# Backward attention loop: dQ of two query chunks packed in one PSUM bank by key tiles with zero columns, and a new loop order

## The chip, the cores and the metric

The kernel runs on one core of one Trainium2 chip. A core has a matrix engine (TensorE, PE in the profile), a vector engine (DVE), an activation engine (ACT), a general engine (POOL) and a queue engine that only issues DMAs (SP). PE writes its results into PSUM, eight banks of 128 partitions x 512 fp32. The metric is the device time of one execution in microseconds; the profile is one execution.

## The reference

One transformer block, forward and backward, for a sequence of 2048 tokens with 512 features, in bf16: layer norm with modulation, self-attention with 32 heads of 16 features, output projection, a second layer norm and an MLP with squared ReLU; then the gradients of the input, the weights and the modulation for a given `grad_out`. The core of what matters here:

```python
qkv = (x @ wqkv).reshape(B, S, 3, H, Dh) ...          # H = 32, Dh = 16
scores = jnp.einsum('bhqd,bhkd->bhqk', q, k) * Dh ** (-0.5)
p = _softmax(scores, axis=-1)
o = jnp.einsum('bhqk,bhkd->bhqd', p, v)
...
_out, _vjp = jax.vjp(_f, A_x, A_wqkv, A_wo, ...)
_grads = _vjp(grad_out)
```

In the backward pass of the attention, with P the softmax and dO the gradient at its output, dV = P^T dO, dS = P * (dO V^T - delta), dK = dS^T Q and dQ = dS K.

## The kernel before

The program runs in stages: preparation of q, k and v; the forward attention with the dense layers of finished query chunks in between; the dense backward layers of the last chunk; the backward attention loop (lines 1557 to 1776), to which the change belongs; and a last stage that turns and multiplies the gradients (lines 1778 to 1998). Tensors between the stages are kept in DRAM: `q_st` holds q by groups of four heads, `k_st` (line 89) holds k by tokens, all heads side by side.

The backward loop works on eight groups of four heads. Within a group it goes through four chunks of 512 keys (kc), and within each through four chunks of 512 queries (qc); one such pair is a block, 128 blocks in all. A block is four units of 128 queries. For a unit and a head:

- `score` (line 1596, token s): one matmul makes 128 x 512 scores in one of three PSUM banks, called A, B and C. Its operands use 32 of PE's rows; the four heads of a group lie on four different groups of rows.
- `expo` (line 1606, token e): ACT takes the exponential from the bank into E_u.
- `dp_pair` (line 1611, token D): for two heads at once, two matmuls make dO V^T - delta in psD_u, a pair of banks (two such pairs exist), and DVE multiplies by E_u into dS_u. This is a product in what follows; a block has eight.
- `k_quad` and `v_quad` (lines 1657 and 1666, token q): four matmuls each add the unit to dK and dV in one bank, accVK.
- `transpose_unit` (line 1632): for dQ the products must be turned. SP issues DMA transposes of dS_u into dsT: for two units at a time (line 1640, 1.05 MB), and in odd blocks for units 0 and 1 at a time and for unit 2 alone (line 1638, half the size). Unit 3 of odd blocks is turned by PE instead (`pe_turn`, line 1649, tokens t) and copied by ACT (tokens T, line 1769).
- `dq_quad` (line 1682, token d): for each of the four key tiles of a block, four matmuls, one per head, multiply the turned products with k. The weights are 32 columns of KS_tok, which holds k by tokens for all heads: 16 columns of the head and the 16 columns after them. So each head's 32 rows of the bank (dqacc, which takes bank C's place) hold 16 rows of dQ and 16 rows that nobody reads.
- `dq_out` (line 1693, token Q): ACT copies the bank out; for the first key chunk to dQacc (line 1700), for later ones to dqtmp (line 1703), which POOL adds (line 1708). At a head group's end its dQ is stored by four DMAs (line 1712).

The order of the work is written out by hand. Two lists of tokens (lines 1714 to 1722), one for iterations after an odd block (`order_t`) and one for the others (`order_n`), are played in turn; the letters beside them give the bank of each score. The order of the tokens sets the order on each engine; engines run their own lists in order and wait for each other by semaphores. The counters nD and nq (line 1732) say which product and which quad a D or q token stands for; nD starts at -1, so products lag one token behind. An iteration b does the scores of block b, turns the PE part of block b-1, and multiplies dQ of block b-2. PE also gets small dummy matmuls (`keep_warm`, line 1645, token f).

ACT's queue also issues DMAs: `plan_head` (line 1587) spreads the loads of the next head group over the loop, one every four products, and stores go the same way. POOL spreads q of the next group into place (`spread_qz`, line 1221). KS_tok is filled once, ahead of the loop, by four DMAs (lines 1370 to 1373).

Of the kernel before, what the change touches and what calls it, by code (L numbers as in the profile page):

```python
# [20 lines left out]
P = 128  # L21
# [8 lines left out]
EPS = 1e-5  # L30
QPAD = 528


@with_exitstack
def kernel(
# [111 lines left out]
    with ExitStack() as ph:  # L147
# [848 lines left out]
        def plan_tasks():  # L996
# [72 lines left out]
            def token_tile(which, g, ti):  # L1069
                key = (which, g)  # L1070
                if ti == 0:
                    T[key] = cb.tile([P, 4, D], BF, name="tokP", tag=htags[(g if which == 0 else g + 1) % 3])
                t = 4 * g + ti
                pt = pools["mm"].tile([P, 4, P], BF, name="ptk", tag="pm")
                for b in range(4):
                    src = sP[:, 4 + 4 * (g % 2) + b, ti * P:(ti + 1) * P] if which == 0 else KTs[b][:, t * P:(t + 1) * P]
                    PE.transpose(pt[:, b, :], src, identb[:])
                gs = slice(4 * g, 4 * g + 4)
                if which == 1:
                    DVE.tensor_copy(T[key][:, ti, :], pt.rearrange("p b q -> p (b q)"))  # L1080
                    if ti == 3:
                        later(1, sp, k_st[:, gs, :], T[key][:])
                else:
                    tok = T[key].rearrange("p t d -> p (t d)").rearrange("p (g t e) -> p g t e", g=HG, t=4)
                    DVE.tensor_copy(tok[:, :, ti, :], pt.rearrange("p b q -> p (b q)").rearrange("p (g e) -> p g e", g=HG))
                    if ti == 3:
                        later(1, sp, q_st.rearrange("g p t e -> p g t e")[:, :, gs, :], tok)

# [132 lines left out]
        def spread_qz(hg):  # L1221
# [3 lines left out]
            else:  # L1225
                POOL.tensor_scalar(to, fro, SCALE, None, ALU.mult)

        def tick():
# [13 lines left out]
        def last_chunk(O_c, L, w1T, w2T):  # L1242
# [301 lines left out]

    KS_tok, dOs_tok = keep["KS"], keep["dOs"]
    qz1pool = tc.alloc_tile_pool(name="qz1pool", bufs=1, side="right")
# [10 lines left out]
    with ExitStack() as ph:  # L1557
# [9 lines left out]
        def load_head(hg):  # L1567
            st = dict(hsets[hg % 2])
            st["qz"] = qz[hg % 2]
            st["acc"] = stg.tile([P, n], F32, name="dQacc", tag="dQacc", bufs=1)  # L1570
            st["dq"] = stg.tile([P, n], BF, name="dQst", tag="dQst", bufs=1)
            st["vk"] = stg.tile([P, n], BF, name="vkb", tag="vkb")
            hst[hg] = st


        todo = {}
# [29 lines left out]
        def expo(u, hq):  # L1606
            if hq == 0:
                bst[u] = [ework.tile([P, 4, 512], BF, name="E_u", tag="E_u"), None]
# [36 lines left out]
        def keep_warm():  # L1645
            PE.matmul(cur["vk"][0:DH, :], KS_tok[:, 0, D:QPAD], dOs_tok[:, 0, :], start=False, stop=False,
                      tile_position=(0, 0), skip_group_check=True)
# [34 lines left out]
        def dq_quad(b, kt):  # L1682
            hg, kc, qc, _ = units[4 * b]
            if kt == 0:
                cur["dq"] = psx.tile([P, 512], F32, name="dqacc", tag="px")
            acc = cur["dq"]
            tT = dqt[b]
            for hq in range(4):
                h = hg * 4 + hq
                PE.matmul(acc[32 * hq:32 * hq + 32, :], KS_tok[:, kc * 4 + kt, h * DH:h * DH + 32], tT[:, :, hq * 4 + kt, :],  # L1690
                          start=(kt == 0), stop=(kt == 3), tile_position=(0, 32 * hq), skip_group_check=True)

        def dq_out(b):
            hg, kc, qc, _ = units[4 * b]
            acc = cur["dq"]
            del dqt[b]
            st = hst[hg]
            dst = st["acc"][:, qc * 512:(qc + 1) * 512]
            if kc == 0:
                ACT.activation(dst, acc[:], AF.Identity, scale=SCALE)  # L1700
            else:
                tmp = wk.tile([P, 512], F32, name="dqtmp", tag="dqtmp")
                ACT.activation(tmp[:], acc[:], AF.Identity, scale=SCALE)  # L1703
                if kc == QC - 1:
                    dst2 = st["dq"][:, qc * 512:(qc + 1) * 512]
                else:
                    dst2 = dst
                POOL.tensor_tensor(dst2, dst, tmp[:], ALU.add)  # L1708
            if kc == QC - 1 and qc == QC - 1 and hg < HG - 1:
                for hq in range(4):  # L1710
                    r = hg % 2 * 64 + hq * DH
                    at(cur["j"] + 6 + hq, load, dQc[hg // 2, r:r + DH, :], st["dq"][32 * hq:32 * hq + DH, :])

        order_t = (
# [3 lines left out]
            "s15 q q e15 ").split(), "ABCABBABACABABCA"  # L1718
# [10 lines left out]
        with tc.manual_schedule(engines={PE.engine, ACT.engine, DVE.engine, SP.engine, POOL.engine}):  # L1729
            head_fill(1)  # L1730
            POOL.memset(qz[1][:], 0.0)
            nD, nq = -1, -4
            idle = psx.tile([P, 512], F32, name="idle", tag="accVK")
            for b in range(NU // 4 + 3):
                toks, bank = order_t if on_pe(b - 1) else order_n
                for tok in toks:
# [38 lines left out]
            assert not todo  # L1775
        dq_last = hst[HG - 1]["dq"]

    with ExitStack() as ph:
# [281 lines left out]
```

## Time and profile before

| | |
|---|---|
| time of the runs, median (lowest to highest) | 2516.67 us (2509.24 to 2526.46), 3 runs |
| profiled execution, span | 2517.6 us |
| PE busy | 2342.5 us, 93% |
| ACT busy | 2302.3 us, 91% |
| DVE busy | 1810.1 us, 72% |
| POOL busy | 350.0 us, 14% |
| first and last exponential of the backward loop | start at 1125.3 and 2379.8 us |
| last dQ matmuls | start at 2389.8 us |

The span is the time from the first to the last instruction of the profiled execution; it is within a microsecond of the median of the runs. Shares are averages over all stages. A PE or ACT instruction overlaps the one after it, so their busy shares say less than the distance between the starts of successive instructions. In a line of the timeline the first number is the start in us from the span's start, the second the length of the instruction or of a merged run of like ones (x3 is three of them), and in brackets stands how long the engine was idle before it and what released it. In a line of the costliest groups stand the number of instructions, the busy time in us, the mean of one in ns, and the idle time before them. SPq and ACTq are the queues' own instructions, such as the issue of a DMA.

### The profile page before, as it was taken

To read this page: it belongs to the slowest core of one execution; us is meant where nothing else is said; L and a number is where in the kernel's file an instruction comes from. 1 tells how busy PE (TensorE), PEld (TensorE's weight loads), DVE (VectorE), ACT (ScalarE), POOL (GpSimd) and SP (SyncE) were. 2 spreads that over 40 slices of the span, in tenths; PEclk is the share of its full clock that TensorE was granted. 3 is DMA by queue.
4 is the path that set the end of the run, shared out by engine and by line. 5 is a ranking of instruction groups with operands and counts; after the bars stand their busy time and mean duration, and the time that the engine had idled before them with its cause. 6 is when DMAs were issued, how large, how long until landed. Compare 5 with 4: busy or idle time off the path is not lost. (4 is left out here: it accounts for less than half of the span.)

```text
span 2517.6 us, 49897 instructions
## 1 busy us (share of the span) xinstructions
PE 2342.5 (93%) x19005; PEld 776.3 (31%) x19005; DVE 1810.1 (72%) x2341; ACT 2302.3 (91%) x3577; POOL 350.0 (14%) x379
## 2 busy tenths in 40 slices
PE   7899889989988999999999999999999999999999
PEld 3232223222322323442233322233323323322343
DVE  5556153454435454579999999999999999998862
ACT  7999999999989999539999999999999999999842
POOL 2000000211323142210111101111010111100100
PEclk9999999999999999999999999999999999998999
DMA  6476455367658766979999999999999999999972
GB/s 202 136 193 165 150 122 139 96 161 144 103 85 176 151 134 119 261 208 191 202 199 210 196 206 208 201 207 202 207 202 202 209 195 203 195 208 212 196 237 72
DMA packets 1220981, 447.15 MB, mean 178 GB/s; under 512 B 1096951, under 2 KB 1191607, under 8 KB 1220486
## 3 DMA queue, kind: packets, MB, share of 16 engines
q1 hardware_dynamic: 1192822, 409.11, 82.2%
q0 software_dynamic: 10944, 16.78, 4.8%
q10 hardware_dynamic: 16976, 18.07, 2.8%
q8 instruction: 149, 2.44, 0.4%
q14 instruction: 90, 0.74, 0.1%
HBM read 96.75 MB, written 73.95 MB: 68 GB/s over the span
## 5 line engine op out<-in xcount | busy, mean ns | idle before, releaser
L1625 DVE TENSOR_TENSOR dS_u<-psD_u,E_u 128x1024 bf16<-128x1024 f32 x1024 | 1186.0, 1218 | 71.6 <-PE psD_u L1623 24.0
L567 ACT ACTIVATE ET<-psST 128x1024 bf16<-128x1024 f32 x1024 | 942.0, 1260 | 27.0 <-PE psST L565 26.5
L1609 ACT ACTIVATE E_u<-psS_A 128x512 bf16<-128x512 f32 x768 | 513.1, 668 | 10.5 <-PE psS_C L1603 8.5
L1609 ACT ACTIVATE E_u<-psS_B 128x512 bf16<-128x512 f32 x768 | 505.8, 659 | 12.1 <-DMA dsT<-dS_u 3.0
L1623 PE MATMUL psD_u<-iv,ido 32*128 32x512 bf16 x2048 | 409.6, 388 | 0.0
L565 PE MATMUL psST<-qt_sb,kt_sb 32*128 32x512 bf16 x2048 | 317.8, 387 | 62.0 <-ACT ET L567 46.6
L1609 ACT ACTIVATE E_u<-psS_C 128x512 bf16<-128x512 f32 x512 | 335.4, 655 | 3.3 <-PE psS_B L1603 1.4
L1603 PE MATMUL psS_B<-ik,iq 32*128 32x512 bf16 x768 | 295.3, 385 | 12.8 <-ACT E_u L1609 5.5
L1603 PE MATMUL psS_A<-ik,iq 32*128 32x512 bf16 x768 | 293.4, 382 | 10.9 <-DVE dwlast L237 1.0
L1603 PEld LDWEIGHTS <-iq 32*128 32x128 bf16 x2048 | 130.2, 91 | 316.1 <-issue 298.8
L1663 PE MATMUL accVK<-dS_u,qz 128*32 128x512 bf16 x2048 | 213.3, 390 | 0.4 <-PE psD_u L1623 0.2
L581 PE MATMUL oacc<-ET,vaug 128*32 128x512 bf16 x2048 | 207.7, 396 | 2.2 <-DVE ostage L585 2.2
L1672 PE MATMUL accVK<-E_u,dOs_tok 128*16 128x512 bf16 x2048 | 204.1, 387 | 0.0
L1708 POOL TENSOR_TENSOR dQacc<-dQacc,dqtmp 128x512 f32<-128x512 f32 x64 | 81.2, 1268 | 852.0 <-ACT dqtmp L1703 852.0
L1603 PE MATMUL psS_C<-ik,iq 32*128 32x512 bf16 x512 | 194.7, 380 | 4.2
L565 PEld LDWEIGHTS <-kt_sb 32*128 32x128 bf16 x2048 | 85.8, 91 | 352.2 <-issue 324.6
L1690 PE MATMUL dqacc<-dsT,KS_tok 128*32 128x512 bf16 x2048 | 146.5, 384 | 18.5 <-DMA dsT<-dS_u 4.3
L1769 ACT ACTIVATE dsT<-ptT 128x1024 bf16<-128x1024 bf16 x128 | 145.8, 1139 | 7.9 <-PE ptT L1653 7.3
L251 DVE COPY part<-pm 128x512 f32<-128x512 f32 (+2 forms) x103 | 63.5, 617 | 114.8 <-PE pm L233 111.5
L1623 PEld LDWEIGHTS <-ido 32*128 32x128 bf16 x2048 | 104.6, 91 | 98.9 <-issue 92.9
L1663 PEld LDWEIGHTS <-qz 128*32 128x32 bf16 x2048 | 58.4, 94 | 177.9 <-issue 162.9
L581 PEld LDWEIGHTS <-vaug 128*32 128x32 bf16 x2048 | 53.1, 93 | 121.4 <-issue 121.4
(407 smaller groups left out, 2516.3 us busy)
## 6 DMA issues: line engine op xcount, KB each, us to landing
p_st<-part POOLq DMA_DIRECT2D x36, 256.0 KB, 5.2
kt_sb<-qkT_st SPq DMA_DIRECT2D x124, 64.0 KB
wA<-in_B_w_dram SPq DMA_DIRECT2D x28, 256.0 KB
wB<-w1T_st SPq DMA_DIRECT2D x21, 256.0 KB
wA<-w2T_st SPq DMA_DIRECT2D x21, 256.0 KB
wB<-in_B_w_dram SPq DMA_DIRECT2D x21, 256.0 KB
p_st<-part POOLq DMA_DIRECT2D x25, 192.0 KB, 5.3
p_st<-part SPq DMA_DIRECT2D x18, 256.0 KB
```

Of the source, the lines that this page charges most:

```text
L565: PE.matmul(ps[:, hi, :], kt_sb[r:r + 32, kt * P:(kt + 1) * P], qt_sb[r:r + 32, :], start=True, stop=True, tile_position=(r, 0))
L567: ACT.activation(ET[:, 2 * pair:2 * pair + 2, :], ps[:], AF.Exp, scale=SCALE)
L581: PE.matmul(oacc[32 * hq:32 * hq + 32, :], lhsT, ET[:, hq, :], start=(kt == 0), stop=(kt == TT - 1), tile_position=(0, 32 * hq), skip_grou ...
L1603: PE.matmul(psS[:], st["q"][r:r + 32, qt * P:(qt + 1) * P], st["k"][r:r + 32, kc * 512:kc * 512 + 512], start=True, stop=True, tile_positi ...
L1609: ACT.activation(bst[u][0][:, hq, :], sst.pop((u, hq))[:], AF.Exp, scale=SCALE)
L1623: PE.matmul(psD[:, hi, :], st["do"][r:r + 32, qt * P:(qt + 1) * P], st["v"][r:r + 32, kc * 512:kc * 512 + 512], start=True, stop=True, til ...
L1625: DVE.tensor_tensor(dS_u[:, 2 * pair:2 * pair + 2, :], psD[:], E_u[:, 2 * pair:2 * pair + 2, :], ALU.mult)
L1663: PE.matmul(cur["vk"][32 * hq:32 * hq + 32, :], hst[hg]["qz"][:, qt, hq, :], bst[u][1][:, hq, :], start=(qt == 0), stop=False, tile_positi ...
L1672: PE.matmul(acc[32 * hq:32 * hq + DH, :], dOs_tok[:, qt, (hg * 4 + hq) * DH:(hg * 4 + hq + 1) * DH], E_u[:, hq, :], start=False, stop=(qt ...
L1690: PE.matmul(acc[32 * hq:32 * hq + 32, :], KS_tok[:, kc * 4 + kt, h * DH:h * DH + 32], tT[:, :, hq * 4 + kt, :], start=(kt == 0), stop=(kt ...
L1708: POOL.tensor_tensor(dst2, dst, tmp[:], ALU.add)
L1769: ACT.activation(dst, pt[:], AF.Identity)
```

## The change

k is stored and loaded by head groups: `k_st` gets the layout of `q_st`, and in the preparation k's tiles are copied the way q's are. In place of KS_tok there are two buffers KZ, for even and odd head groups. A row of KZ is 144 wide: 16 zeros, then for each of four heads its 16 columns of k and 16 zeros. A memset writes the zeros once; `spread_k` on POOL puts in the k of the next head group, which one DMA per group (on ACT's queue) loads into a staging area.

`dq_quad` takes 32 columns of KZ that begin at a head's columns of k for an even block and 16 before them for an odd one. So an even block's dQ comes out in the first 16 rows of the head's 32 and adds zero to the last 16; an odd block's does the reverse. Two blocks, that is two query chunks, are summed in one bank over eight key tiles, and `dq_out` runs once for both. dQacc and dQst are half as wide, and the stores per head group are eight DMAs (`dq_rows`) for four; so are the last ones, on SP, in the last stage.

All dQ work now lies in the iterations of `order_t`: d1 and d2 stand for the even block b-2, d3 and d4 for the odd block b-1. The lists of tokens are new: nine D tokens and four q tokens in `order_t`, seven and twelve in `order_n`; exponentials no longer go in the order of the heads; nD starts at -2. `keep_warm` takes its zeros from another tile. The loop has 129 iterations in place of 131.

```diff
-    k_st = dram.tile([P, TT, D], BF, name="k_st")
+    k_st = dram.tile([HG, P, TT, 64], BF, name="k_st")
...
+            if hg > 0:
+                yield keep["kst"], k_st[hg]
...
+        def spread_k(hg):
+            to = keep["KZ"][hg % 2][:, :, DH:DH + 128].rearrange("p t (h e) -> p t h e", h=4)[:, :, :, 0:DH]
+            POOL.tensor_copy(to, keep["kst"].rearrange("p t (h d) -> p t h d", h=4))
...
-            keep["KS"] = kpool.tile([P, TT, QPAD], BF, name="KS_tok", tag="ks")
-            POOL.memset(keep["KS"][:, :, D:QPAD], 0.0)
-            for i in range(4):
-                later(4 + 3 * i, sp, keep["KS"][:, 4 * i:4 * i + 4, 0:D], k_st[:, 4 * i:4 * i + 4, :])
+            kz = kpool.tile([P, 2 * TT * KW + TT * 64], BF, name="KZ_tok", tag="ks")
+            POOL.memset(kz[:, 0:2 * TT * KW], 0.0)
...
+            later(4, sp, keep["kst"], k_st[0])
+            later(12, spread_k, 0)
...
+        def dq_rows(dst, hg, src):
+            for hq in range(4):
+                r = hg % 2 * 64 + hq * DH
+                for x in range(2):
+                    yield (dst[r:r + DH, :].rearrange("r (m x c) -> r m x c", x=2, c=512)[:, :, x, :],
+                           src[32 * hq + DH * x:32 * hq + DH * x + DH, :].rearrange("r (m c) -> r m c", c=512))
...
+            at(j0 + 44, spread_k, hg)
...
-            if kt == 0:
-                cur["dq"] = psx.tile([P, 512], F32, name="dqacc", tag="px")
-            acc = cur["dq"]
+            if "dq" not in cur:
+                cur["dq"] = [psx.tile([P, 512], F32, name="dqacc", tag="px"), 0]
+            acc, k = cur["dq"]
+            cur["dq"][1] += 1
             tT = dqt[b]
             for hq in range(4):
-                h = hg * 4 + hq
-                PE.matmul(acc[32 * hq:32 * hq + 32, :], KS_tok[:, kc * 4 + kt, h * DH:h * DH + 32], tT[:, :, hq * 4 + kt, :],
-                          start=(kt == 0), stop=(kt == 3), tile_position=(0, 32 * hq), skip_group_check=True)
+                lo = 32 * hq + DH * (1 - b % 2)
+                PE.matmul(acc[32 * hq:32 * hq + 32, :], KZ[hg % 2][:, kc * 4 + kt, lo:lo + 32], tT[:, :, hq * 4 + kt, :],
+                          start=(k == 0), stop=(k == 7), tile_position=(0, 32 * hq), skip_group_check=True)
...
-            dst = st["acc"][:, qc * 512:(qc + 1) * 512]
+            m = slice(qc // 2 * 512, qc // 2 * 512 + 512)
+            dst = st["acc"][:, m]
...
         order_t = (
-            "s0 s1 q s2 e0 e1 D s3 D e2 s4 e3 t1 e4 q T1 D "
-            "s5 s6 e5 f f t2 e6 s7 T2 e7 D s8 e8 D f f s9 e9 q q s10 "
-            "s11 e10 D d1 d2 e11 Q q s12 D e12 s13 e13 q s14 D e14 "
-            "s15 q q e15 ").split(), "ABCABBABACABABCA"
+            "s2 e2 D s1 e1 s3 e3 f q D s0 e0 s4 e4 D t1 T1 q f s8 D s5 e5 e8 f f s7 e7 s6 e6 "
+            "D q s9 e9 t2 T2 D s11 e11 s10 e10 D q d1 d2 s13 e13 D s12 e12 d3 d4 Q s14 e14 D s15 e15 ").split(), "BABCAAACBBBABAAB"
         order_n = (
-            "s0 D s1 q e0 q s2 e1 e2 D s3 s4 q s5 e3 D e4 "
-            "e5 s6 q s7 D s8 e6 e7 d1 e8 s9 D d2 e9 q Q s10 "
-            "s11 e10 D q s12 e11 e12 s13 e13 D q s14 s15 e14 e15 D q ").split(), "CBACBACBABABCABC"
+            "q q s1 e1 D s0 e0 q s2 e2 D s3 e3 q s5 e5 D s4 e4 q q s7 e7 s6 D s9 e9 e6 q q "
+            "s14 e14 D s8 e8 q s11 e11 s15 e15 D q s10 e10 s12 e12 D s13 e13 q q ").split(), "ACBCBAACBBBAACCC"
...
-            nD, nq = -1, -4
+            nD, nq = -2, -4
...
-            for b in range(NU // 4 + 3):
+            for b in range(NU // 4 + 1):
...
-                        for kt in (2 * i - 2, 2 * i - 1):
-                            dq_quad(b - 2, kt)
+                        for kt in (2 * ((i - 1) % 2), 2 * ((i - 1) % 2) + 1):
+                            dq_quad(b - 2 + (i - 1) // 2, kt)
...
-        for h in range(4):
-            SP.dma_start(out=xs["dq", 3][64 + DH * h:64 + DH * h + DH, :], in_=dq_last[32 * h:32 * h + DH, :])
+        for to, fro in dq_rows(xs["dq", 3], HG - 1, dq_last):
+            SP.dma_start(out=to, in_=fro)
```

More of the change, by code (lines that the diff above doesn't have):

```diff
@@ L30 @@
 EPS = 1e-5
-QPAD = 528
+KW = 2 * DH * 4 + DH
 @with_exitstack
@@ L1078, in token_tile @@
                 gs = slice(4 * g, 4 * g + 4)
[L1079 to L1087, printed above, removed]
+                to = k_st if which == 1 else q_st
+                tok = T[key].rearrange("p t d -> p (t d)").rearrange("p (g t e) -> p g t e", g=HG, t=4)
+                DVE.tensor_copy(tok[:, :, ti, :], pt.rearrange("p b q -> p (b q)").rearrange("p (g e) -> p g e", g=HG))
+                if ti == 3:
+                    later(1, sp, to.rearrange("g p t e -> p g t e")[:, :, gs, :], tok)
             for t in range(4, TT):
@@ L1543 @@
         dwr.release()
-    KS_tok, dOs_tok = keep["KS"], keep["dOs"]
+    KZ, dOs_tok = keep["KZ"], keep["dOs"]
     qz1pool = tc.alloc_tile_pool(name="qz1pool", bufs=1, side="right")
@@ L1606, in expo @@
         def expo(u, hq):
-            if hq == 0:
+            if u not in bst:
                 bst[u] = [ework.tile([P, 4, 512], BF, name="E_u", tag="E_u"), None]
@@ L1645, in keep_warm @@
         def keep_warm():
-            PE.matmul(cur["vk"][0:DH, :], KS_tok[:, 0, D:QPAD], dOs_tok[:, 0, :], start=False, stop=False,
+            PE.matmul(cur["vk"][0:DH, :], zeros[:], dOs_tok[:, 0, :], start=False, stop=False,
                       tile_position=(0, 0), skip_group_check=True)
@@ L1704, in dq_out @@
                 if kc == QC - 1:
-                    dst2 = st["dq"][:, qc * 512:(qc + 1) * 512]
+                    dst2 = st["dq"][:, m]
                 else:
@@ L1770 @@
                     elif c == "d" and 0 <= b - 2 < NU // 4:
-                        for kt in (2 * i - 2, 2 * i - 1):
-                            dq_quad(b - 2, kt)
+                        for kt in (2 * ((i - 1) % 2), 2 * ((i - 1) % 2) + 1):
+                            dq_quad(b - 2 + (i - 1) // 2, kt)
                     elif c == "Q" and 0 <= b - 2 < NU // 4:
                         dq_out(b - 2)
-            assert not todo
+            assert not todo and nD >= 2 * NU and nq >= 2 * NU
         dq_last = hst[HG - 1]["dq"]
```

18 lines of the change are left out of this document (10 added, 8 removed).

## The prediction, made before the changed kernel was run

> **What bounds the kernel now.** I read the page first (shares, slices, costliest groups), then the timeline of DVE, the timeline of SP, and the chain that ended last.
>
> ```profile
> span 2517.6 us, 49897 instructions
> PE 2342.5 (93%) x19005; PEld 776.3 (31%) x19005; DVE 1810.1 (72%) x2341; ACT 2302.3 (91%) x3577; POOL 350.0 (14%) x379
> DVE  5556153454435454579999999999999999998862
> DMA  6476455367658766979999999999999999999972
> L1625 DVE TENSOR_TENSOR dS_u<-psD_u,E_u 128x1024 bf16<-128x1024 f32 x1024 | 1186.0, 1218 | 71.6 <-PE psD_u L1623 24.0
> L1690 PE MATMUL dqacc<-dsT,KS_tok 128*32 128x512 bf16 x2048 | 146.5, 384 | 18.5 <-DMA dsT<-dS_u 4.3
> L1708 POOL TENSOR_TENSOR dQacc<-dQacc,dqtmp 128x512 f32<-128x512 f32 x64 | 81.2, 1268 | 852.0 <-ACT dqtmp L1703 852.0
> ```
>
> The slices show the backward loop as the right half: DVE and the DMA share at nine tenths. The change lives there. Its 1024 DVE products cover 1186.0 us and DVE waits 71.6 us between them: 1257.6 us, half the span. The loop repeats every two blocks (16 products; 64 such periods): 1257.6/64 = 19.65 us, of which 18.5 are DVE work. So an ideal order saves at most 71.6 us.
>
> Timeline of DVE in mid-loop:
>
> ```profile
> 1500.62 7.23 DVE L1625 TENSOR_TENSOR dS_u<-psD_u,E_u 128x1024 bf16<-128x1024 f32 x6 [0.24 <-PE psS_A L1603]
> 1508.22 11.45 DVE L1625 TENSOR_TENSOR dS_u<-psD_u,E_u 128x1024 bf16<-128x1024 f32 x10 [0.37 <-ACT dqtmp L1703]
> 1519.91 7.23 DVE L1625 TENSOR_TENSOR dS_u<-psD_u,E_u 128x1024 bf16<-128x1024 f32 x6 [0.24 <-PE psS_A L1603]
> ```
>
> 16 products in 19.29 us; ten in a row take 11.45, so the pitch is 1.13 to 1.15. DVE is nearly the wall already. ACT is a second wall: successive exps start 0.475 us apart in its timeline (1499.54, 1500.01, 1500.49), 32 of them are 15.2, two copies of turned tiles 0.9 each, two dQ evacuations about 0.5 each, half a dV/dK evacuation 0.25: 18.3 of 19.3.
>
> Timeline of SP, which issues only transposes here:
>
> ```profile
> 1661.39 16.83 SPq L1640 DMA_TRANSPOSE dsT<-dS_u  x3
> 1678.31 3.39 SPq L1638 DMA_TRANSPOSE dsT<-dS_u  x1
> 1681.79 16.32 SPq L1640 DMA_TRANSPOSE dsT<-dS_u  x3
> 1698.21 2.88 SPq L1638 DMA_TRANSPOSE dsT<-dS_u  x1
> 1701.26 15.98 SPq L1640 DMA_TRANSPOSE dsT<-dS_u  x3
> 1717.33 3.06 SPq L1638 DMA_TRANSPOSE dsT<-dS_u  x1
> 1720.48 15.94 SPq L1640 DMA_TRANSPOSE dsT<-dS_u  x3
> ```
>
> Per period three whole transposes (about 5.4 us each) and a half one (1.7 to 4.8, median 2.59): 18.7 us of SP in 19.3. This third wall does not show in the engine shares. It costs nothing today because dQ of block b is multiplied two iterations later, after the data has long landed: the page gives PE only 4.3 us of waiting for it. When a half transpose lands is seen twice, in the chain that ended last:
>
> ```profile
> 2307.44 6.26 DMA dsT<-dS_u
> 2313.83 1.05 PE dqacc L1690 x8
> ...
> 2383.76 3.11 SPq L1638
> 2389.02 8.03 DMA qz<-dQc
> ```
>
> The first was issued at 2307.44 and released PE at 2313.8, 6.4 us later; the second, issued at 2383.76, released the last dQ matmuls at 2389.1, 5.4 later.
>
> **The change part by part.**
>
> *Evacuations of dQ.* 128 of them (96 dqtmp, 32 dQacc; 0.6 us each, 0.5 of pitch) become 64: 32 us less ACT work, 0.5 per period. ACT falls to 17.8, below DVE's 18.5, so it gains at most the waits that it causes. POOL loses 48 adds of 1.27 and gains eight spreads of k (the like spread of q takes 2.77): POOL is idle 86% of the time, worth 0.
>
> *Zero columns.* The matmul count stays 2048 and each still streams 512 columns into 32 rows; zeros take the place of columns of the next head, whose product nobody read. Worth 0.
>
> *Set-up.* A memset of 4608 columns for one of 256: by the 1.80 us of 2048 columns, 4.1 us for 0.31, on a POOL that waits 45.8 us right after. k is stored in shorter runs, as q is (DVE copies 425 against 424 ns). One 0.26 MB load for four of 0.5 MB. Worth 0; between -1 and +2.
>
> *ACT's DMA issues.* Per head one load of k more and eight dQ stores for four, 35 issues of 0.31 in all. The issue at 1501.88 lies between two ACT instructions 0.48 apart, so they hide: 0; at most 11 us.
>
> *The order.* Let X be the end of the product after which the half transpose is asked for (product 13 of a period). In the old order thirteen more products are issued before the odd block's first dQ matmul; with PE two products ahead of DVE that is at least 12 us. In the new one d3, d4 for that block stand in the very next iteration after eight products, of which PE can issue the eighth when the sixth is done: PE gets there at X+7 to X+8.5 (the scores ahead of it need exps too). They wait for both transposes of the odd block. Behind them on PE stand s14, product 6's matmuls and s15, so DVE and ACT run dry behind that wait.
>
> When does the half transpose land? The new order puts seven products into the second iteration, and they ask for a whole transpose after the first of them, another after the fifth, and the half one after the seventh: SP needs 13 us for what DVE asks for in 7.9. This closes a loop, in which every step waits for the one before:
> d3 and d4, 16 matmuls, until product 6's matmuls start: 1.0 (the x16 group at 1506.49 covers 1.05);
> those matmuls to the start of the product: 0.5 (0.39 for the pair, and a semaphore);
> products 6 and 7: 2.35 (2 x 1.13 and the last one's drain);
> two whole transposes on SP: 10.9 (two thirds of 16.3, the mean of the x3 rows between 1600 and 1755, gaps in);
> the half one from issue to landing: 5.4 (of 5.4 and 6.4, the smaller: the shortest issues take 1.7, the 5.4 had 3.1).
> Sum 20.15 us a period. It exceeds DVE's 18.5, ACT's 17.8 and SP's 19.0 (18.7 and four gaps of 0.09), so it sets the pace. Bounds: with the shortest rows (4.77 twice, the half one 1.70 and a tail of 2.3, 5.4 less 3.1) 17.6, which no longer binds; with 5.6 twice (a third of 16.83) and 6.4, 21.6.
>
> Loop: 63 x 20.15 + 18.5 = 1288 against 1257.6: +30. The old loop's mean of 19.65 is 0.36 above the quiet stretch shown, 23 us in all; part of that are stretches where PE's granted clock drops:
>
> ```profile
> 2300.00:2350.00 50.00, 46.95 (x427) 14.21 (x425) 43.31 (x38) 45.22 (x86) 5.07 (x4) 0.86 1.10 196
> ```
>
> (a stretch by engine, then PE's clock, 0.86 where quiet ones have 1.00). In the new loop PE's wait covers most of such losses, so I add 4 (bounds 0 and 23).
>
> *Tail.* The last dQ leaves by eight DMAs for four, 0.58 to 1.15 each on SP; PE waits 5.3 us for the last of that stage's loads, so they are on the path: +2.4 (bounds 0 and +4.6).
>
> Sum: +36 on a span of 2517.6, 2554; that execution is 1 us above the median of 2516.67. I give 2552.
>
> A rule against this. The SP row first: 1.05 MB per whole transpose in 5.4 us is 194 GB/s. The Trainium skill, DMA: Bandwidth & Descriptors, section Latency and other measured facts, has 261 GB/s for such transposes, 350 to 400 if contiguous. By that, an estimate: 4.0 us each and 4.3 for the half one would make the loop 16.4 and the new wait vanish; the rows of this loop, 192 of them between 4.77 and 6.83, decide.
>
> **The rivals.**
>
> *Faster, no wait.* The half transpose lands by X+8.5, about when PE comes there. Then SP itself paces: 19.05 x 64 = 1219, -38 and +2: 2482. For it: ACT and PE have slack, and transposes that meet fewer loads are shorter. Against it: all of SP's rows above. It decides from a loop sum under 19.2, 0.95 us less than mine. That is 15%. If the transposes also ran at their shortest rows (16.0 a period), DVE would pace at 18.5 to 18.9: 2450 to 2470; 5%. By the Trainium skill's figure above this would be the outcome.
>
> *No difference.* The wait binds, but the loop sum is about 19.6 because heads without loads (last quarter of each head) have shorter transposes: what ACT loses is what DVE waited for before. 19.6 x 64: 2520; 28%.
>
> *Slower still.* Three banks minus the one that dQ holds leave scores with two while PE waits; ACT, stopped for 2 us, has 18 exps to make before the next period's first product, 8.6 us, and vk's evacuation. If that adds 0.8 a period: 21.0 x 64 = 1344, 2600; 7%.
>
> **How the numbers follow.** Forecast 45%, own range 2535 to 2575. The range reaches to the no-wait rival and most of the slow one: 2475 to 2590; outside lie the 5% below and about half of the slow rival, and the forecast's and rivals' edges. Over 1% is what a measurement of this kernel can tell (25 us): faster, below 2491, is the two rivals, 0.20; within 1% the 28% and no more, 0.28; slower 0.52.
>
> **What would show it.** Right: PE's dQ group waits for the DMA dsT in nearly every period, 1 to 2 us each (60 to 130 us in all); DVE's idle time grows towards 100 us with psD as releaser; SP issues 20 us apart; ACT's evacuations of dQ number 64. Wrong: SP rows of 4.8 us, or that wait seen in few periods; then the pace is 19 or less. It would also be wrong if DVE idles with ACT's exps as releaser instead.

## The result, and the profile after

The changed kernel takes 2589.94 us (median of 4 runs, 2587.77 to 2601.31) against 2515.37 us for the kernel before (4 runs, 2509.24 to 2526.46): ratio 1.0304, 95% interval 1.0269 to 1.0338. That is slower by some 75 us; the forecast was 2552, slower by 36. The profiled execution's span is 2586.0 us, 68.4 more than before's 2517.6.

The page of the changed kernel, the lines that answer to those shown of before:

```profile
span 2586.0 us, 49558 instructions
...
PE 2356.2 (91%) x19004; PEld 750.0 (29%) x19004; DVE 1814.8 (70%) x2341; ACT 2273.7 (88%) x3513; POOL 300.8 (12%) x339
...
DVE  5646153454435445679989899899898998888962
...
L1637 DVE TENSOR_TENSOR dS_u<-psD_u,E_u 128x1024 bf16<-128x1024 f32 x1024 | 1190.3, 1217 | 141.9 <-PE psS_B L1615 60.7
...
L1703 PE MATMUL dqacc<-dsT,KZ_tok 128*32 128x512 bf16 x2048 | 143.9, 403 | 65.1 <-DMA dsT<-dS_u 54.4
...
L1723 POOL TENSOR_TENSOR dQacc<-dQacc,dqtmp 128x512 f32<-128x512 f32 x32 | 40.6, 1267 | 698.8 <-ACT dqtmp L1718 698.8
```

In the loop's half of the slices many of before's nines have become eights. The products work as long as before (1190.3 us), but DVE waits 141.9 us between them, twice the 71.6. PE's dQ group waited 4.3 us for turned products; now it waits 54.4. ACT does 28.6 us less work and POOL half the adds: that part came as the change says, and neither bought time.

From the start of the first product to the end of the last the loop takes 1329.5 us, 1255.8 before: +73.7. It also begins 2.6 us earlier, and the stage behind it is 2.7 us shorter (132.6 against 135.2); 73.7 - 2.6 - 2.7 is the 68.4 of the spans. So the whole loss lies in the loop.

**One period in eight is another.** DVE's timeline, mid-loop, with the end of one head group's dQ in it:

```profile
1652.35 1.23 DVE L1637 TENSOR_TENSOR dS_u<-psD_u,E_u 128x1024 bf16<-128x1024 f32 x1 [4.49 <-PE psD_u L1635]
1654.92 2.35 DVE L1637 TENSOR_TENSOR dS_u<-psD_u,E_u 128x1024 bf16<-128x1024 f32 x2 [1.35 <-PE psD_u L1635]
1657.95 20.00 DVE L1637 TENSOR_TENSOR dS_u<-psD_u,E_u 128x1024 bf16<-128x1024 f32 x17 [0.67 <-PE psS_B L1615]
1678.79 18.70 DVE L1637 TENSOR_TENSOR dS_u<-psD_u,E_u 128x1024 bf16<-128x1024 f32 x16 [0.84 <-PE psS_B L1615]
1698.62 2.42 DVE L1637 TENSOR_TENSOR dS_u<-psD_u,E_u 128x1024 bf16<-128x1024 f32 x2 [1.13 <-PE psS_B L1615]
```

The last two rows are the normal state: a pause of 0.8 to 1.1 us once in a period, at product 6, the first whose operands PE makes behind d3 and d4. The pauses of 4.49, 1.35 and 0.67 us ahead of them are something else. Measured at the same product of successive periods (product 13), 56 of the 63 distances have a mean of 19.95 us (18.83 to 23.75). The other seven, the second of each head group from the second group on, take 24.3 to 28.3 us, 183.7 in sum: 44 us more than seven normal ones. Before, those seven have a sum of 142.1, some 7 us over its quiet 19.25.

The long period as ACT's timeline shows it:

```profile
1644.99 1.20 ACTq L1596 DMA_DIRECT2D dQc<-dQst  x1
1645.36 0.59 ACT L1621 ACTIVATE E_u<-psS_A 128x512 bf16<-128x512 f32 x1
1646.30 1.02 ACT L1780 ACTIVATE dsT<-ptT 128x1024 bf16<-128x1024 bf16 x1 [0.34 <-PE psD_u L1635]
1649.99 0.33 ACTq L1596 DMA_DIRECT2D iqs<-q_st  x1
1650.35 0.57 ACTq L1596 DMA_DIRECT2D dQc<-dQst  x1
1650.97 0.60 ACT L1621 ACTIVATE E_u<-psS_A 128x512 bf16<-128x512 f32 x1 [3.65 <-issue]
```

ACT stands for 3.65 us between a copy and an exponential, and what ends the stop is not an operand: it is the issue of a load, `iqs<-q_st`, among the eight stores `dQc<-dQst`. In the trace's semaphore events the DMAs that SP and ACT issue raise eight semaphores in turn (lanes, below), the transposes among them. This load's lane had last been given to the transpose that SP issued at 1641.72; that one landed at 1649.96, and the load was issued at 1649.99. The exponential behind it in ACT's queue had to wait. The same holds in all seven long periods: the issue that ends the longest stop waits for one semaphore alone, and starts 0.02 us after the landing of the transpose that had it last. The seven stops are 2.5 to 5.2 us long, 26 in sum. The other 18 of the 44 are shorter pauses among the stores and behind the stop.

So the working theory has two losses: *the wait* (d3 and d4 wait for the half transpose; the forecast's loop), and *the lanes* (more DMAs on ACT's queue, each of which may have to wait there until an older DMA of its lane has landed). Rivals: the stops are only the wait seen from ACT; or the new order of scores and exponentials is slower by itself, whatever it waits for.

One more thing in the records belongs to both losses: PE's granted clock, which is 1.00 in a quiet stretch, stands at 0.50 in stretches of 3.4 to 17.1 us. Behind the loop's first two periods these are 14 stretches, 88.7 us in sum, against seven and 34.1 before. Thirteen of the 14 begin during a pause of PE of 1.9 to 5.4 us or at most 1.6 us behind it, and each of the seven long periods has one. Before, five normal periods hold one of 3.4 us, with no pause of PE over 0.9 us ahead of it, and take 20.6 us for 19.25. So a wait here costs its own length and often some time at half the clock behind it. How much of the loss that is, no run separates; by 1.3 us per 3.4 us it is, as an estimate, some 20 us of the 73.7.

### The profile page after: what moved, and what is told of

Read it like the earlier page. It is cut to its first block, busy times and chain, and to the rows that moved or that the text cites. A ratio compares the mean times of both kernels' runs of the same rounds, so it can differ in the third digit from the quotient of the medians.

```text
span 2586.0 us, 49558 instructions
## 1 busy us (share of the span) xinstructions
PE 2356.2 (91%) x19004; PEld 750.0 (29%) x19004; DVE 1814.8 (70%) x2341; ACT 2273.7 (88%) x3513; POOL 300.8 (12%) x339
## 4 chain that ended last, share of the span: by engine, by line
PE 36%; ACT 29%; DMA 14%; DVE 10%; issue 8%; SPq 1%; POOL 1%; ACTq 1%; POOLq 0%; DVEq 0%
ACT E_u L1621 17%; DMA dsT<-dS_u 13%; ACT ET L567 9%; DVE dS_u L1637 5%; PE psST L565 4%; PE dqacc L1703 3%; PE pm L233 3%; PE oacc L581 2%; PE psS_B L1615 2%; PE pm L414 2%; PE pdh L1895 2%; PE pwq L1929 2%; PE pm L400 2%; PE pm L489 1%; PE psS_A L1615 1%
## 5 line engine op out<-in xcount | busy, mean ns | idle before, releaser
L1637 DVE TENSOR_TENSOR dS_u<-psD_u,E_u 128x1024 bf16<-128x1024 f32 x1024 | 1190.3, 1217 | 141.9 <-PE psS_B L1615 60.7
L1621 ACT ACTIVATE E_u<-psS_A 128x512 bf16<-128x512 f32 x768 | 479.2, 624 | 52.6 <-PE psS_B L1615 21.8
L1621 ACT ACTIVATE E_u<-psS_B 128x512 bf16<-128x512 f32 x768 | 482.3, 628 | 18.5 <-DMA out_dram<-xlast 7.3
L1635 PE MATMUL psD_u<-iv,ido 32*128 32x512 bf16 x2048 | 420.1, 395 | 0.1
L1621 ACT ACTIVATE E_u<-psS_C 128x512 bf16<-128x512 f32 x512 | 325.1, 635 | 7.1 <-PE psS_A L1615 2.7
L1675 PE MATMUL accVK<-dS_u,qz 128*32 128x512 bf16 x2048 | 224.6, 400 | 0.2 <-issue 0.2
L1615 PEld LDWEIGHTS <-iq 32*128 32x128 bf16 x2048 | 120.2, 92 | 312.8 <-issue 309.7
L1703 PE MATMUL dqacc<-dsT,KZ_tok 128*32 128x512 bf16 x2048 | 143.9, 403 | 65.1 <-DMA dsT<-dS_u 54.4
L1780 ACT ACTIVATE dsT<-ptT 128x1024 bf16<-128x1024 bf16 x128 | 134.4, 1050 | 8.2 <-PE ptT L1665 6.1
L1723 POOL TENSOR_TENSOR dQacc<-dQacc,dqtmp 128x512 f32<-128x512 f32 x32 | 40.6, 1267 | 698.8 <-ACT dqtmp L1718 698.8
L1658 PE MATMUL accVK<-dOs_tok,zeros 128*16 128x512 bf16 x264 | 92.7, 392 | 0.0
```

Source lines behind the costliest of these rows:

```text
L1615: PE.matmul(psS[:], st["q"][r:r + 32, qt * P:(qt + 1) * P], st["k"][r:r + 32, kc * 512:kc * 512 + 512], start=True, stop=True, tile_positi ...
L1621: ACT.activation(bst[u][0][:, hq, :], sst.pop((u, hq))[:], AF.Exp, scale=SCALE)
L1635: PE.matmul(psD[:, hi, :], st["do"][r:r + 32, qt * P:(qt + 1) * P], st["v"][r:r + 32, kc * 512:kc * 512 + 512], start=True, stop=True, til ...
L1637: DVE.tensor_tensor(dS_u[:, 2 * pair:2 * pair + 2, :], psD[:], E_u[:, 2 * pair:2 * pair + 2, :], ALU.mult)
L1658: PE.matmul(cur["vk"][0:DH, :], zeros[:], dOs_tok[:, 0, :], start=False, stop=False, tile_position=(0, 0), skip_group_check=True)
L1675: PE.matmul(cur["vk"][32 * hq:32 * hq + 32, :], hst[hg]["qz"][:, qt, hq, :], bst[u][1][:, hq, :], start=(qt == 0), stop=False, tile_positi ...
```

## The experiments

Unless said otherwise the edit is to the changed kernel. Medians of before in the four groups of runs are 2518.24, 2517.57, 2517.22 and 2516.22 us.

### The wait taken out, the stores moved, and both

```diff
-            tT = dqt[b]
+            tT = dqt[b - b % 2]
```

d3 and d4 read the even block's turned products, which have landed long before, so dQ of odd blocks is not computed.

> The changed kernel, but d3 and d4 read the turned products of the even block instead of the odd one's, which landed long before (so dQ of odd blocks is wrong; same matmuls, same order, same transposes). Theory: the wait of d3 for the half transpose closes the loop that sets the pace of about 19.9 us a period; without it SP's own issue time paces, about 19.0, so some 0.9 x 63 = 55 us less than the changed kernel: 2535. Rival A: the new order itself (two score banks, bursts on ACT and PE) sets the pace; then no change, 2590. Rival B: all of the loss sits in the eight stretches where ACT stops behind its own DMA issues; then no change either.

Measured: 2556.53 us, ratio 1.0157 (1.0129 to 1.0185), 33 us less than the changed kernel, where 55 were expected. The normal periods fell a little further than expected, nearly all to 18.77 to 18.97 us. But the seven long ones grew, from 26.2 to 29.4 us in the mean. The waits of this kernel, engine, what waits, what for, sum, times and longest:

```profile
ACT E_u L1621 <- DMA dsT<-dS_u: 40.5, 10, 7.3
...
DVE dS_u L1637 <- ACT E_u L1621: 29.3, 13, 7.3
...
PE dqacc L1703 <- DMA dsT<-dS_u: 0.9, 1, 0.9
```

PE's wait for turned products is gone (0.9 us). Yet exponentials, which read no turned product, now wait 40.5 us for those DMAs. ACT's timeline shows where:

```profile
1634.41 0.60 ACT L1621 ACTIVATE E_u<-psS_B 128x512 bf16<-128x512 f32 x1 [5.07 <-DMA dsT<-dS_u]
1634.53 1.19 ACTq L1596 DMA_DIRECT2D dQc<-dQst  x1
1634.91 0.59 ACT L1621 ACTIVATE E_u<-psS_A 128x512 bf16<-128x512 f32 x1
1635.77 1.02 ACT L1780 ACTIVATE dsT<-ptT 128x1024 bf16<-128x1024 bf16 x1 [0.27 <-PE psD_u L1635]
1639.60 0.33 ACTq L1596 DMA_DIRECT2D iqs<-q_st  x1
1639.96 0.56 ACTq L1596 DMA_DIRECT2D dQc<-dQst  x1
1640.57 0.60 ACT L1621 ACTIVATE E_u<-psS_A 128x512 bf16<-128x512 f32 x1 [3.78 <-DMA dsT<-dS_u]
```

Two stops among the stores of one head group. The stops are therefore not the wait of d3 and d4 in another guise.

Next, the stores on POOL's queue, the wait left in:

```diff
+        def store(to, fro):
+            POOL.dma_start(out=to, in_=fro)
...
-                    at(cur["j"] + 6 + i, load, to, fro)
+                    at(cur["j"] + 6 + i, store, to, fro)
```

> The changed kernel with the eight dQ stores of a head group issued on POOL's queue instead of ACT's. Theory: once per head group ACT stands still for 3 to 5 us because the next DMA on its queue has to wait for a semaphore lane that a running transpose holds, and the stores use up the lanes; the period there is 24 to 28 us where others have 19.9. Away from ACT's queue seven such stops go: 35 to 45 us less, 2545 to 2555. Rival: the stop comes from the load of k or from the turn to the next head group; then it stays, 2590.

Measured: 2574.97 us, 1.0221 (1.0179 to 1.0262): only 15 us less. Exponentials no longer wait for any DMA. But the seven periods are still long, 162.8 us in sum for 183.7: in each of them PE's dQ now waits 2.3 to 4.6 us for turned products, 24 us in sum, where in the changed kernel it did not wait for them there. In all, PE's wait for turned products has grown from 50.7 to 76.8 us:

```profile
PE dqacc L1706 <- DMA dsT<-dS_u: 76.8, 48, 4.6
DVE dS_u L1640 <- PE psS_B L1618: 72.1, 52, 5.8
```

While ACT stood, SP's transposes caught up; without the stop they are late again. Each loss covers part of the other, so the size expected here was wrong. With both edits:

> Both edits of the two runs before together (dQ of odd blocks wrong). Theory: the two losses are separate and add: about 90 to 100 us less than the changed kernel, 2490 to 2500, below the kernel before, paced by SP at 19.0 a period. Rival: they cover each other (the stop lets the transposes catch up), then 2530 or more.

Measured: 2526.80 us, 1.0032 (1.0014 to 1.005), 63 less than the changed kernel and nearer the rival's 2530 than the 2490 to 2500 of the theory. It is more than 33 + 15 = 48, as fits two losses that cover each other. 63 is most of the 75 that the change cost. But the kernel is not faster than before, though ACT does less and quiet periods are 18.8: the mean of all is 19.41. SP's timeline in this kernel:

```profile
1473.04 16.25 SPq L1655 DMA_TRANSPOSE dsT<-dS_u  x3
1489.34 3.25 SPq L1653 DMA_TRANSPOSE dsT<-dS_u  x1
1492.76 16.27 SPq L1655 DMA_TRANSPOSE dsT<-dS_u  x3
1509.13 2.54 SPq L1653 DMA_TRANSPOSE dsT<-dS_u  x1
```

The gaps between rows are 0.05 to 0.17 us long: SP is never free, over the loop it issues transposes for 1211.8 of 1253.2 us. The loop is nearly as long as its transposes, 97%.

### Transposes as the wall

The third wall put to the test: the last kernel, and the half transpose of odd blocks not made at all (so dQ of odd blocks is again not computed).

```diff
-                if qi == 2:
-                    SP.dma_start(out=dqt[u // 4][:, qi], in_=bst[u][1].rearrange("p h k -> p (h k)"), transpose=True)
+                pass
```

> Dq of odd blocks multiplies the even block's turned products, stores on POOL's queue, and the half transpose is not made at all (unit 2 of odd blocks is never turned; dQ wrong). Theory: in the run with both edits SP paces with 98% of its time in transposes; without the half one it needs 16.2 us a period, and the loop runs at the 18.8 that its quiet periods show: 64 x 0.6 = 38 us less, about 2485. Rival: PE, ACT and DVE together set 19.4, then no change, 2527.

Measured: 2479.56 us, 0.9846 (0.9821 to 0.9871), 47 less than with them. Nearly all periods are 18.77 to 18.83 (mean 18.86), and DVE's timeline has rows such as this one, 86 products without a pause of 0.2 us:

```profile
1499.87 101.32 DVE L1640 TENSOR_TENSOR dS_u<-psD_u,E_u 128x1024 bf16<-128x1024 f32 x86
```

With nothing late, the new order runs close to DVE's own pace (18.86 us, of which 16 products take 18.6), and behind its first period the clock is never at 0.50 (for 37.5 us with the half transposes). Its scores and exponentials are not slower by themselves: that rival falls.

### More stores in the old order

Does the loss from the lanes belong to the new order? The kernel before, each of its four dQ stores split into two halves, on ACT's queue as they were; nothing else.

```diff
-                    at(cur["j"] + 6 + hq, load, dQc[hg // 2, r:r + DH, :], st["dq"][32 * hq:32 * hq + DH, :])
+                    for x in range(2):
+                        cols = slice(x * n // 2, (x + 1) * n // 2)
+                        at(cur["j"] + 6 + 2 * hq + x, load, dQc[hg // 2, r:r + DH, cols], st["dq"][32 * hq:32 * hq + DH, cols])
```

> The kernel before, with each of its four dQ stores per head group split in two halves, one after each product, on ACT's queue as they were. Theory of the lanes: more DMAs in a short time run into lanes held by transposes in the old order too; 10 to 30 us more, 2527 to 2547. Rival: the old order takes them without loss, 2517, and the stops come from the new order alone.

Measured: 2546.07 us, 1.0112 (1.0075 to 1.0149): +28. The seven long periods are here too, 24.1 to 25.4 us, 173.0 in sum against 142.1 before, 31 more: the whole difference. The same stop is in ACT's waits, where before has one of 3.0 us:

```profile
ACT E_u L1609 <- DMA dsT<-dS_u: 11.1, 5, 3.2
```

So four more DMAs per head group on ACT's queue cost the old kernel nearly as much as the forecast gave to the whole loop, 28 us for 34. The other side of it, the four stores of before moved to POOL's queue:

> The kernel before, with its four dQ stores per head group on POOL's queue. Theory of the lanes: the old order loses at most the few 1 to 3 us stops that its trace shows at these stores: 5 to 15 us less, 2503 to 2513. Rival: POOL's queue delays its own adds, or nothing changes: 2518.

Measured: 2517.72 us, 1.0011 (0.9992 to 1.0031). The 5 to 15 us that the theory expected did not come. The seven periods did fall, from 142.1 to 135.1 us in sum, but the other 56 took 5.4 us more. Four stores cost nothing worth having; eight do.

### dQ later

If the wait is a matter of place, dQ can be put later. First the whole dQ work of two blocks, behind the first product of the next iteration, with bank letters arranged anew:

```diff
-            "D q s9 e9 t2 T2 D s11 e11 s10 e10 D q d1 d2 s13 e13 D s12 e12 d3 d4 Q s14 e14 D s15 e15 ")
+            "D q s9 e9 t2 T2 D s11 e11 s10 e10 D q s13 e13 D s12 e12 s14 e14 D s15 e15 ")
...
-            "q q s1 e1 D s0 e0 q s2 e2 D ...
+            "q q s1 e1 D s0 e0 d1 d2 d3 d4 Q q s2 e2 D ...
...
```

> The changed kernel with its dQ work (d1 to d4 and Q) moved from the end of one iteration to the start of the next, behind product 7 instead of ahead of product 6, banks of the second list renamed so that C is free there, and the dQ stores on POOL's queue. All outputs are computed. Theory: PE now comes to d3 two products later (at X+9 instead of X+7), about when the half transpose lands at X+9.4; the wait shrinks from 1 to 2 us to under 0.5 and the period goes to the 19.4 of the run that did not wait: 2520 to 2540. Rival: the burst stalls ACT at its new place, since the exps of products 8 and 9 stand behind it; then 2560 or more.

> The same later dQ work, with the dQ stores left on ACT's queue. Theory: the stop of ACT behind its own DMA issues, once per head group, stays and grows as the other periods shorten (28 to 30 us for that period): 25 to 35 us above the run with POOL's queue. Rival: with transposes under less pressure the stop goes away; then equal to that run.

Measured: 2718.78 us, 1.0797 (1.078 to 1.0815), with the stores on POOL's queue, and 2739.61, 1.0888 (1.0864 to 1.0912), on ACT's, 21 us above for the 25 to 35 expected. The expectation failed by some 200 us, though the wait did vanish (2.1 us in all). PE's timeline in the first, and its DVE's:

```profile
1705.29 2.34 PE L1706 MATMUL dqacc<-dsT,KZ_tok 128*32 128x512 bf16 x32
1707.45 0.39 PE L1678 MATMUL accVK<-dS_u,qz 128*32 128x512 bf16 x4
1708.39 0.37 PE L1618 MATMUL psS_C<-ik,iq 32*128 32x512 bf16 x1 [0.55 <-ACT dQacc L1718]
```

```profile
1708.89 19.11 DVE L1640 TENSOR_TENSOR dS_u<-psD_u,E_u 128x1024 bf16<-128x1024 f32 x16 [2.17 <-PE psS_A L1618]
1731.51 3.48 DVE L1640 TENSOR_TENSOR dS_u<-psD_u,E_u 128x1024 bf16<-128x1024 f32 x3 [3.50 <-PE psS_A L1618]
```

32 matmuls in one burst take 2.34 us here, in which PE makes no scores, and the next score into bank C waits for the copy that empties it. DVE idles 3.05 us in the mean at that place; the period is 22.76.

But the row shown is a short one. The bursts take from 1.91 us, at a granted clock of 1.00, to 3.6 at 0.50, 3.5 in the median, and most run largely at 0.50. In this row of the same kernel the numbers behind the engines' are PE's clock, the DMA share and GB/s:

```profile
1700.00:1800.00 100.00, 90.19 (x774) 25.37 (x774) 81.18 (x70) 82.07 (x152) 6.28 (x4) 0.86 0.99 175
```

The clock is at 0.50 for 307 us in sum, and 62 of its 63 periods hold such a stretch; the one without takes 21.04 us. So the move replaced the wait by something dearer, of which the burst and bank C are one part and the clock another. What lowers the clock at the burst isn't shown.

Then only d3, d4 and Q two products later, d1 and d2 left in place:

```diff
-            ... d1 d2 s13 e13 D s12 e12 d3 d4 Q s14 e14 D s15 e15 ")
+            ... d1 d2 s13 e13 D s12 e12 s14 e14 D s15 e15 ")
...
-            "q q s1 e1 D s0 e0 q s2 e2 D ...
+            "q q s1 e1 D s0 e0 d3 d4 Q q s2 e2 D ...
...
```

> The changed kernel with its dQ stores on POOL's queue, and with d3, d4 and Q alone put two products later: behind the first product of the next iteration (d1 and d2 stay; the bank letters of that iteration are rearranged, since dqacc holds bank C into it). Theory (the wait is a matter of place: d3 and d4 stand too close behind the half transpose; two products later takes 2.3 us out of the loop of waits, 19.95 becomes 17.7, which no longer binds, and 16 matmuls in a burst cost at most 1.05 us, which PE's lead of two products hides): PE waits less than 20 us in all for turned products, SP paces, periods of 19.0 to 19.4, 2505 to 2530 us. Rival (as with the whole dQ work moved: what comes behind the burst and behind Q's copy is the next scores and exponentials, so DVE idles there instead): periods of 20 or more, 2560 us or more.

> The same with the dQ stores left on ACT's queue as in the changed kernel: only the place of d3, d4 and Q differs from it. Theory of two separate losses (wait and lanes): 15 to 40 us above the run with the stores on POOL's queue, from one long period per head group. Rival (the stop of ACT's queue matters only while the loop is tight, and a later place of d3 and d4 leaves slack to catch up): within 10 us of it.

Measured: 2561.15 us, 1.018 (1.0152 to 1.0208), on POOL's queue, and 2595.36, 1.031 (1.0283 to 1.0336), on ACT's. On the wait the theory was right, and on the time the rival. The waits of the first:

```profile
PE psS_A L1618 <- ACT E_u L1624: 42.6, 63, 0.7
...
DVE dS_u L1640 <- PE psD_u L1638: 29.1, 50, 2.9
...
DVE dS_u L1640 <- ACT E_u L1624: 18.2, 66, 2.8
...
PE dqacc L1706 <- DMA dsT<-dS_u: 2.5, 4, 1.3
```

Turned products are on time now (2.5 us). But once in each period, 63 times, PE's next score waits 0.7 us for an exponential to empty bank A, since dqacc holds bank C into the next iteration and two banks are left. The pace of 19.86 to 19.99, the same in nearly every period and at a clock of 1.00, comes with it; that the banks alone make it is argued from this row, not shown. The two runs differ by 34 us, and the long periods are back in the second: 178.1 us in sum, 39 over seven of 19.92. This is the lanes' price again, at a place where no wait for turned products covers it.

### Less to transpose

Last, a version meant to beat both: PE turns heads 2 and 3 of unit 2 as well, so that the half transpose becomes a quarter, at the price of one more copy on ACT per period.

```diff
+            if qi == 2 and on_pe(u // 4):
+                held["dS2"] = dS_u
...
-                    SP.dma_start(out=dqt[u // 4][:, qi], in_=bst[u][1].rearrange("p h k -> p (h k)"), transpose=True)
+                    SP.dma_start(out=dqt[u // 4][:, qi, 0:8], in_=bst[u][1][:, 0:2].rearrange("p h k -> p (h k)"), transpose=True)
...
-                PE.transpose(pt[:, i, :], held["dS"][:, 2 * half + i // 4, kt * P:(kt + 1) * P], identb[:])
-            dst = dqt[b][:, 3, 8 * half:8 * half + 8, :]
+                src = held["dS2"][:, 2 + i // 4] if half == 2 else held["dS"][:, 2 * half + i // 4]
+                PE.transpose(pt[:, i, :], src[:, kt * P:(kt + 1) * P], identb[:])
+            dst = dqt[b][:, 2, 8:16, :] if half == 2 else dqt[b][:, 3, 8 * half:8 * half + 8, :]
...
-            ... s8 D s5 e5 e8 f f s7 e7 s6 e6 "
+            ... s8 D s5 e5 e8 t3 T3 f f s7 e7 s6 e6 "
```

> The changed kernel with its eight dQ stores on POOL's queue, and with one more quarter of an odd block turned by PE: heads 2 and 3 of unit 2 (one group of PE transposes and one copy on ACT per period), so that the half transpose is halved again. Theory (three walls: SP's transposes, the wait for the last of them, the stores ahead of ACT's queue): SP falls from about 19.0 to about 17.8 us a period, the last transpose lands about 1.3 us earlier, PE's dQ waits nearly vanish, ACT rises by one copy of 0.9 us; periods of 18.8 to 19.0, 2485 to 2505 us. Rival (ACT becomes the wall, since its copy is put among the exponentials that products wait for): periods of 19.4 or more, 2520 to 2540 us, with DVE idle behind the exponentials instead of behind the turned products.

> The same with the dQ stores left on ACT's queue, as in the changed kernel. Theory (lanes: one period in eight is longer, since a DMA at the head of ACT's queue waits until an older transpose or store of its lane has landed): 15 to 35 us above the run with the stores on POOL's queue, one period in eight of 23 us or more. Rival (with shorter transposes the lanes come free in time): within 8 us of it.

Measured: 2575.52 us, 1.0224 (1.0196 to 1.0252), on POOL's queue, and 2623.57, 1.0416 (1.0387 to 1.0446), on ACT's. The first half of the theory holds: SP needs 17.4 to 18.6 us a period (16.09 and 1.26, 16.39 and 2.13, and the gap) and rests for 2.8 us between the two, where the kernel before had 0.1 to 0.2:

```profile
1692.21 16.09 SPq L1657 DMA_TRANSPOSE dsT<-dS_u  x3
1708.40 1.26 SPq L1655 DMA_TRANSPOSE dsT<-dS_u  x1
1712.47 16.39 SPq L1657 DMA_TRANSPOSE dsT<-dS_u  x3
1728.96 2.13 SPq L1655 DMA_TRANSPOSE dsT<-dS_u  x1
```

PE's wait for turned products falls to 7.8 us. But the period is 20.25 to 20.32, and the time is above the rival's 2520 to 2540 too:

```profile
DVE dS_u L1640 <- PE psD_u L1638: 97.8, 131, 2.0
...
PE psS_C L1618 <- ACT dsT L1786: 48.1, 63, 1.0
...
PE dqacc L1709 <- DMA dsT<-dS_u: 7.8, 7, 1.9
```

The extra copy empties bank C 0.8 us too late for the next score in it, once a period, and DVE then pauses 1.17 us. Once a period, then, the copy on ACT and its bank cost more than SP's wall did. With the stores on ACT's queue the price of the lanes is 48 us, more than the 15 to 35 expected and the largest of the pairs.

## Why the prediction failed, and what in it was right

**The wait: right; its sum: near in the mean, in part by luck.** The forecast had 20.15 us a period; normal periods have a mean of 19.95. The terms of the sum can be read off the rows. SP's timeline of the changed kernel:

```profile
1671.62 3.55 SPq L1650 DMA_TRANSPOSE dsT<-dS_u  x1
1675.61 16.74 SPq L1652 DMA_TRANSPOSE dsT<-dS_u  x3
1692.44 2.22 SPq L1650 DMA_TRANSPOSE dsT<-dS_u  x1
1695.14 16.71 SPq L1652 DMA_TRANSPOSE dsT<-dS_u  x3
1711.95 3.17 SPq L1650 DMA_TRANSPOSE dsT<-dS_u  x1
```

From the issue of the half transpose (1671.62, 1692.44) to product 6 (1678.79, 1698.62 in DVE's rows above) it is 7.17 and 6.18 us; the sum had 5.4 + 1.0 + 0.5 = 6.9. Products 6 and 7 end at 1701.04, and two whole transposes and the gaps bring SP to 1711.95, 10.9 later, as in the sum. Taking the wait out brought quiet periods of 18.8, so it was the wait that set the pace. But it is not one pace. The waits run from 0.1 to 3.3 us; 49 of the 56 normal periods have a mean of 19.60, and seven, with waits of 1.9 to 3.3 us and half the clock behind them, take 21.9 to 23.75. The forecast said that PE's wait would cover most of the clock's losses and added 4 us; here half the clock comes behind the waits. A smaller wait and a dearer clock together gave a mean near the forecast's. Against before's mean of 19.56 over the same 63 distances the order costs 63 x 0.39 = 25 us; the forecast had 34 for the loop.

**What it said would show it: right in part.** SP's groups start 19.4 to 20.1 us apart, and dQ's evacuations are 64. PE waits for turned products 43 times, 50.7 us, where it had 60 to 130, in nearly every period. DVE's releaser is mostly the scores (psS_B, 60.7 us) and not psD. DVE's idle time is 141.9 us, not "towards 100", and that was the sign of something unforeseen.

**The step that failed: "ACT's DMA issues".** It counted 35 more issues, looked at one that hid between two instructions, and gave "0; at most 11 us", 0.31 each. The stores' issues are longer than that, 0.56 to 1.62 us, but most of their price is not issue time. A DMA at the head of ACT's queue can wait for an older DMA, and everything behind it on ACT waits too. The seven long periods are 44 us over normal ones: four times the bound. So the forecast's 36 us became 75. The same count of stores costs 28 us in the old order, and the four pairs that differ only in the stores' queue and have little wait for turned products left differ by 30, 34, 48 and 21 us. Before had two signs: the second period of each head group takes 19.7 to 23.1 us there, for 19.25, and its page has a line in which an exponential, which reads no turned product, waits 3.0 us for one:

```profile
L1609 ACT ACTIVATE E_u<-psS_B 128x512 bf16<-128x512 f32 x768 | 505.8, 659 | 12.1 <-DMA dsT<-dS_u 3.0
```

**Terms that hid behind each other.** 25 and 44 are together 69 of the loop's 73.7. They are not prices of removal: taking out the one gains 33, the other 15, both 63.

**The tail: wrong in sign, without weight.** +2.4 was given for eight stores on SP; that stage came out 2.7 us shorter.

**The rivals.** "No wait" fell with SP's rows. A whole transpose takes 5.25 us in the mean, 200 GB/s, and took 5.33 before. The 261 GB/s of the Trainium skill, DMA: Bandwidth & Descriptors, section Latency and other measured facts, are not reached by either. Had the wait been absent, that rival's 19.05 a period would still have been too low: the kernel with neither loss has 19.41, SP's own sum with its longer transposes in it, and takes 2526.80, not 2482. "Slower still" expected 2600 from another place, scores with two banks; that mechanism appears in the kernel with d3 and d4 later. The result, 2589.94, lies outside the forecast's own 2535 to 2575 and at the very edge of the range of 2475 to 2590. That the wide range holds it is luck: the room was made for that rival, not for the step that caused the loss.

No kernel here that computes all outputs beats the one before. Left open: whether the version with the quarter transpose would with its copy at another place and other bank letters, since its SP has some 2 us to spare in a period; that wasn't tried.

## What to carry to other kernels

Count a DMA that is put on a compute engine's queue not by its issue time alone but by what it may have to wait for there, and ask what that engine was about to do; the price appears once per burst and is easily missed in a quiet stretch. Walls that lie close together (here products at 18.5 us, ACT, and transposes at 19) make each repair worth less than the wait that it removes: read off the next wall before moving work to get past this one. And a burst moved out of the way of a late transfer still takes its engine's time and its bank: where it lands, the next score waits. Read the granted clock beside every such pause, too: here the time behind a wait was often spent at half of it.

## What the runs showed of the hardware

- DMAs issued by SP and by ACT raise eight semaphores in turn, and an issue was held until the older DMA of the same semaphore had landed (load at 1649.99, transpose landed at 1649.96), with compute work of ACT behind it stopped for 2.5 to 5.2 us in the changed kernel and up to 7.3 in the one without the wait. Stores issued on POOL's queue showed no such stop of ACT.
- The changed kernel's dQ stores take 0.56 to 1.62 us of ACT's queue per issue, 0.64 in the median; before's take 0.31 to 1.84, 0.36 in the median, and most loads there 0.31 to 0.33.
- A quarter-size transpose (0.26 MB) takes SP 1.26 to 2.13 us, the half one 2.2 to 3.6 in the rows shown: about in proportion to their bytes.
- In the loop the granted clock is 1.00 or 0.50. Behind the first two periods it stood at 0.50 for 88.7 us in the changed kernel, 34.1 before, 307 with the burst of 32 matmuls and not at all without the half transpose. Thirteen of the changed kernel's 14 stretches begin during a pause of PE of 1.9 us or more or just behind it; five of the seven before, and those of the burst's kernel between 1400 and 1700 us, have no pause of PE over 0.9 us ahead of them.
